# Half of w_out2 converted in the second phase, w_in over five batches, and the fifth transposition and first taps of the first batch ahead of val

## The chip, the cores and the metric

The kernel runs on one core of one Trainium2 chip. The metric is the device time of one execution in microseconds (us). The engines named are TensorE (PE), VectorE (DVE), ScalarE (ACT), GpSimd (POOL) and SyncE (SP), which issues all the DMAs.

## The reference

There are eight batches of 576 tokens by 512 features. Each batch goes through three layers:

```
kv   = k^T v per head;  o = q kv;  x = o / rms(o) * g_norm        # 8 heads of 64
gate = sigmoid(causal 5-tap convolution of x along the tokens)
y    = (gate * (x @ w_val)) @ w_out
h    = gelu(y @ w_in);  u, v = halves of h
v_s  = w_sg @ layernorm(v) + b_sg                                 # mixes the tokens of a batch
out  = y + (u * v_s) @ w_out2
```

The matrices w_val, w_out, w_in (512 x 1024) and w_out2 come in double precision.

## The kernel before, in words

**Products.** Each operand of a large product is split into a high and a low part, and a 128-row block of a result is twelve PE products (`gemm3`, L195 to L213: high by high, high by low, low by high, four slices of the contraction each). A weight is such a pair of tiles: WV for w_val, WO for w_out, wiv and wiu for the two halves of w_in, K and V for w_out2.

**Conversion of the weights.** Double precision arrives as pairs of 32-bit integers. `split` (L131) loads one piece (L148) and makes the parts with a chain over several engines: ACT L117 and DVE L127, then DVE L128 and L120, ACT L162 (the high part), DVE L129 and L124, POOL L167 (DVE for the first weights), DVE L169 (the low part). A piece of w_in or w_out2 is 128 x 256; w_in has 16 pieces, w_out2 has 8. Their raw integers lie in the two buffers of `raw`, their temporaries in the one buffer of `cv`. The phase-2 loads of tokens (L425) and of the gathered tokens (L541) take the same two buffers of `raw`.

**Phase 1**, per batch: kv (L252), o (L268) in five steps of 128 tokens (the fifth has 64), the root mean square (DVE L275 and L278, POOL L279 and L280), its scaling (DVE L283), the transposition on PE (L298), whose result ACT copies to the high part X0h or X1h (L302) and to X (L303) and DVE makes the low part of (L307); the convolution (`taps`: ACT L326; `conv`: DVE L332, sixteen instructions per batch), the sigmoid (ACT L335), `val` (PE L201, `val<-X0h,WV`), the gate (DVE L360, ACT L361, DVE or POOL L364), `out` (PE L201, `y<-Z,WO`), ACT L378 and the store to y_main (L380). The last 64 tokens of four batches are gathered and run as one more such block ("the rest", XR and GR).

**Phase 2**, per batch: the tokens of y are loaded back (L425), split by ACT L428 and DVE L429, multiplied with the v half of w_in (`hv`, PE L451), go through the gelu (ACT L436 and L440, DVE L437 and L441) and the normalisation (DVE L460 to L466, POOL L463, DVE L492); the u half is `hu`. `sg` (PE L560) mixes tokens, its eviction (DVE L561) scales and adds b_sg, which the tile bsg holds; `gated` (DVE L571, ACT L572, DVE L576) and `wout2` (PE L201, `out<-Z,K`) follow. X and `rem` belong to the remaining 64 tokens of each batch (ACT L519, DVE L520).

**What sets the order.** The opening, up to the second conversion of w_out, is written out by hand (L666 to L726). `busy(n)` there issues n idle products on PE (`warm`, two instructions each). After it the program is a list of closures: `later(slots, fn, rank)` puts one behind the next matrix products, `tick` runs those that are due, and `behind(marks, fn)` ties a conversion behind instructions that were issued three steps ago; a scheduler then orders each engine's queue. In batches 2 to 5 each odd step s converts one piece of w_in (L766). w_out2 takes the odd steps of batch 6 and steps 0 to 3 of batch 7 (L771 to L780). `background(pieces, every, first)` (L609) converts a list one by one, every so many ticks.

Of the kernel before, what the change touches and what calls it, by code (L numbers as in the profile page):

```python
# [10 lines left out]
F32R = mybir.dt.float32r  # L11
# [8 lines left out]
P = 128  # L20
B, S, D, DH = 8, 576, 512, 64
NK = D // P
# [38 lines left out]
def body(ctx, tc, qT, k, v, gcol, w_val, conv_w, w_out, w_in, g_ln, w_sgT, b_sg, w_out2, out, out_r):  # L61
# [8 lines left out]
    def sb(tag, shape, dtype=F32, bufs=1):  # L70
        count[0] += 1
        return pool.tile([P] + shape, dtype, tag=tag, name=f"{tag}_{count[0]}", bufs=bufs)
# [117 lines left out]
                for c in range(0, n, WC) for kt in range(NK)]  # L190

    wv = sb("WV", [2, NK, D], F32R)
    wo = sb("WO", [2, NK, D], F32R)

    def gemm3(ps, w, m, xh, xl):  # L195

        msl = slice(m * P, (m + 1) * P)
        i = 0
        for kt in range(NK):
            for a, x in ((w[0], xh), (w[1], xh), (w[0], xl)):  # L200
                nc.tensor.matmul(ps, lhsT=a[:, kt, msl], rhs=x[:, kt],  # L201
                                 start=(i == 0), stop=(i == 3 * NK - 1))
                i += 1
# [11 lines left out]
    def busy(n):  # L215
        for i in range(n):
            nc.tensor.matmul(warm[:, :P], lhsT=ident, rhs=ident, start=True, stop=True)
# [126 lines left out]
    class Moe:  # L344
# [26 lines left out]
        def out(self, m):  # L371
            if m == 0:
                self.y = sb("Y", [NK, self.n])
            ps = bank("y", self.n)
            gemm3(ps, (wo[:, 0], wo[:, 1]), m, self.z[:, 0], self.z[:, 1])

            def done():
                act(self.y[:, m], ps, AF.Copy)  # L378
                if m == NK - 1:
                    dma(self.dst, self.y)  # L380

            later(0, done, 1)
# [247 lines left out]
    spare = sb("Y", [2, 2 * D], I32)  # L630

    def first_weight(w, src, raws):
        return [split(src[:, m * P:(m + 1) * P], w[:, 0, :, m * P:(m + 1) * P], w[:, 1, :, m * P:(m + 1) * P],
                      raws[m], first[1][:, m % 2], NK, False)
                for m in range(NK)]

    wv_pieces = first_weight(wv, w_val, [first[0][:, i] for i in range(4)])
    wo_pieces = first_weight(wo, w_out, [spare[:, 0], spare[:, 1], first[0][:, 0], first[0][:, 1]])
    att = Attention(0)
    atts = [att, Attention(1)]  # L640
# [25 lines left out]
    with tc.manual_schedule():  # L666
        for m in range(NK):
            wv_pieces[m][0]()
        wo_pieces[0][0]()
        att.load_kv()  # L670
        dma(gcol_s, gcol)
        dma(gln_s, g_ln)
        cw_work = taps()
        att.load_q()
        atts[1].load_kv()
        wo_pieces[1][0]()
        atts[1].load_q()
        in_turn(wv_pieces[0], wv_pieces[1])
        in_turn(wv_pieces[2], wv_pieces[3])
        wo_pieces[2][0]()  # L680
        wo_pieces[3][0]()
        busy(27)
        att.kv(0)
        busy(5)
        att.kv(1)
        busy(4)
        in_turn(wo_pieces[0])
        slots.drain()
        cw_work()
        steps = [att.o(t, None) for t in range(5)]  # L690
        lows = []
        for t in range(5):
            steps[t][0](ts)
            if t >= 2:
                steps[t - 2][1]()
                busy(4)
                lows.append(steps[t - 2][2]())
            if t == 4:
                lows[0]()
        for t in (3, 4):  # L700
            steps[t][1]()
            if t == 3:
                busy(4)
                lows.append(steps[t][2]())
            lows[t - 2]()
        lows[3]()
        moe = Moe(att.xh, att.xl, gate, y_main[0])
        z = [moe.val(0, True)]
        steps[4][2]()
        for m in range(NK):  # L710
            att.taps(m)
        z.append(moe.val(1, True))
        atts[1].kv(0)
        atts[1].kv(1)
        slots.drain()
        z += [moe.val(m, True) for m in (2, 3)]
        for a in (0, 2):
            att.conv((a, a + 1))
            att.sigmoid(a)
            att.sigmoid(a + 1)  # L720
        for m in range(NK):
            z[m][0]()
        for m in range(NK):
            z[m][1](False)
        in_turn(wo_pieces[1])
    marks = [latest()]  # L726
    atts.append(Attention(2))
    atts[2].load_kv()

    for b in range(B):  # L730
        if b:
            moe = Moe(atts[b].xh, atts[b].xl, gate, y_main[b])
        nxt = atts[b + 1] if b + 1 < B else None
        nn = atts[b + 2] if b + 2 < B else None
        if b == 2:
            p2["wiv"], p2["wiu"] = (sb(n, [2, NK, D], F32R) for n in ("wiv", "wiu"))
            wi = split_weight(p2["wiv"], w_in, D, D) + split_weight(p2["wiu"], w_in, 0, D)
            wi[0][0]()
            wi[1][0]()
            wi_n = 0  # L740
        for s in range(8):
            if s < 4:
                if b:
                    moe.val(s)
            else:
                moe.out(s - 4)
            if b == 0 and s in (3, 4):
                later(0, lambda s=s: behind(marks[0], wo_pieces[s - 1][1]), 3)
            if b == 0 and s < 2:
                nxt.o(s)  # L750
            if nxt and s < 3:
                nxt.o(s + 2)
            if nn and s in (3, 4):
                nn.kv(s - 3)
            if nn and s == 3:
                nn.load_q()
            if b + 3 < B and s == 5:
                atts.append(Attention(b + 3))
                atts[-1].load_kv()
            if nn and s in (6, 7):  # L760
                nn.o(s - 6)
            if nxt and s in (5, 7):
                later(0, lambda a=nxt, m=s - 5: a.gates((m, m + 1)), 2)
            if s == 2:
                later(0, atts[b].rest_parts, 2)
            if b in (2, 3, 4, 5) and s % 2:  # L766
                later(0, lambda w=wi[wi_n][1], m=marks[-3]: behind(m, w), 3)
                if wi_n + 2 < len(wi):
                    later(0, wi[wi_n + 2][0], 4)
                wi_n += 1  # L770
            if b == B - 2 and s == 0:  # L771
                w2 = w2_pieces()
                w2[0][0]()
                w2[1][0]()
                w2_n = 0
            if (b == B - 2 and s % 2) or (b == B - 1 and s < 4):
                later(0, lambda w=w2[w2_n][1], m=marks[-3]: behind(m, w), 3)
                if w2_n + 2 < len(w2):
                    later(0, w2[w2_n + 2][0], 4)
                w2_n += 1  # L780
            if b == B - 1:
                if s == 0:
                    v_alloc()
                if s == 4:
                    stage = sb("X32", [NK, S])
                    dma(stage, w_sgT[:4 * P, :].rearrange("(t p) s -> p t s", p=P))
                    toks = Tokens(0)
                    toks.load(0)
                if s > 4:
                    toks.load(s - 4)  # L790
                    later(0, lambda t=s - 5: toks.split(t), 1)
            tick()
            marks.append(latest())
        if b % RG == RG - 1:
            moe = Moe(rest["x"][:, 0], rest["x"][:, 1], rest["g"], y_rest[b // RG])
            for s in range(8):
                if s < 4:
                    moe.val(s)
                else:
                    moe.out(s - 4)  # L800
                if b == B - 1:
                    if s == 0:
                        toks.split(3)
                    if s < 4:
                        toks.hv(s)
                    if s == 2:
                        rem = Rests(0)
                        later(1, rem.split, 1)
                    if s == 4:
                        sg_weight(stage)  # L810
                        rest_weight()
                        p2["r"] = sb("X32", [2, 2, D], F32R)
                        p2["bsg"] = sb("cv", [S])
                        dma(p2["bsg"], b_sg.to_broadcast([P, S]))
                    if s == 5:
                        y_r = Group.load(0)
                if b == B - 1 or s % 2:
                    tick()

    rem = rem.hv()  # L820
    grp = Group(0, y_r)
    tick()
    for b in range(B):
        more = b + 1 < B
        if b % RG == 0:
            if b:
                grp = Group(b // RG, Group.load(b // RG))
            ggr = sb("WO", [2, NK, RW], F32R)
            for m in range(NK):
                grp.hu(m)  # L830
                tick()
# [88 lines left out]
```

## Time and profile before

| | before |
|---|---|
| median of 3 runs | 770.35 us (769.9 to 770.45) |
| the profiled execution | 770.46 us |
| its span in the trace | 768.7 us |
| mean granted TensorE clock | 0.979 |
| busy: PE, DVE, ACT, POOL | 734.5, 589.6, 348.6, 152.7 us |

The busy times are sums over the span, which holds stages with different limits: the opening (to some 40 us), the first two batches (to some 100 us), the other batches of phase 1, the passage to phase 2 (at some 325 to 335 us) and phase 2. A row of the timeline has the start, the duration, the engine, the line, the operation and its tiles, and in brackets the time that the engine sat idle before and what ended it. The granted clock stands as a share of 2.4 GHz.

### The profile page before, as it was taken

How to read it: one execution, taken by the hardware profiler on the slowest of the kernel's cores; microseconds unless marked ns; L12 is line 12 of the kernel's file. 1: busy time of each engine (PE TensorE's matmuls, PEld its weight loads, DVE VectorE, ACT ScalarE, POOL GpSimd, SP SyncE). 2: the span in 40 equal slices, each digit the busy share in tenths (PEclk: the TensorE clock that was granted, in tenths of full speed). 3: DMA queues.
4: the chain of work that ended last, by engine and by line, in shares of the span. 5: the costliest groups of instructions: out<-in, count | busy, mean ns of one | idle time of the engine just before them, and what ended most of it. 6: DMA issues, size and time to landing. Idle time of an engine off the chain costs nothing.

```text
span 768.7 us, 11720 instructions
## 1 busy us (share of the span) xinstructions
PE 734.5 (96%) x4472; PEld 630.0 (82%) x4472; DVE 589.6 (77%) x1137; ACT 348.6 (45%) x662; POOL 152.7 (20%) x163
## 2 busy tenths in 40 slices
PE   6897999999899999859999999999999999999997
PEld 6785878778778787759988988889899888898896
DVE  7799959898779899759976687776875867867662
ACT  3567455655545765526543343433432423434320
POOL 0404425282344462311100000000000000100000
PEclk8998999999999999979999999999999999999999
DMA  9944153536134311342122022121321221121203
GB/s 298 319 136 174 55 181 109 185 123 206 59 129 163 104 69 69 127 144 92 60 61 104 28 70 83 55 79 38 118 91 47 70 96 43 67 70 42 96 1 110
DMA packets 56200, 80.15 MB, mean 104 GB/s; under 512 B 3664, under 2 KB 29264, under 8 KB 55120
## 3 DMA queue, kind: packets, MB, share of 16 engines
q1 hardware_dynamic: 56144, 79.40, 30.8%
q8 instruction: 35, 0.57, 0.3%
q14 instruction: 21, 0.17, 0.1%
HBM read 60.51 MB, written 18.87 MB: 103 GB/s over the span
## 4 chain that ended last, share of the span: by engine, by line
PE 83%; DVE 8%; DMA 4%; POOL 2%; issue 1%; ACT 1%; SPq 0%; DVEq 0%; POOLq 0%
PE sg L560 16%; PE hv L451 13%; PE out L201 12%; PE hu L201 11%; PE val L201 11%; PE y L201 10%; DVE G L332 4%; PE kv L252 3%; PE o L268 3%; PE xT L298 2%; PE hur L201 1%; DMA V<-in_v_dram 1%; DMA Q<-in_qT_dram 1%; POOL st L280 1%; DMA raw<-in_w_in_dram 1%
## 5 line engine op out<-in xcount | busy, mean ns | idle before, releaser
L201 PE MATMUL y<-Z,WO 128*128 128x512 f32 (+1 forms) x480 | 115.8, 389 | 3.0 <-DVE WO L169 2.8
L332 DVE SCALAR_TENSOR_TENSOR G<-X,cw,G 128x576 f32<-128x576 f32 x128 | 99.5, 821 | 9.2 <-ACT G L326 9.2
L201 PEld LDWEIGHTS y<-Z,WO 128*128 128x128 f32 x480 | 84.3, 194 | 20.1 <-DVE WO L169 3.2
L451 PE MATMUL hv<-wiv,X1h 128*128 128x512 f32 x256 | 84.0, 394 | 10.1 <-ACT X1h L428 10.1
L463 POOL TENSOR_TENSOR bmv<-bmv,mhalf 128x1 f32<-128x1 f32 x36 | 21.7, 603 | 348.2 <-DVE bmv L462 337.5
L201 PE MATMUL out<-Z,K 128*128 128x512 f32 x256 | 82.9, 389 | 0.0
L201 PE MATMUL hu<-X1h,wiu 128*128 128x512 f32 x256 | 79.5, 391 | 0.0
L280 POOL TENSOR_TENSOR st<-st,mhalf 128x8 f32<-128x8 f32 (+1 forms) x40 | 69.9, 1754 | 25.4 <-DVE st L279 23.0
L440 ACT ACTIVATE T<-T 128x512 f32<-128x512 f32 x68 | 42.9, 631 | 52.3 <-DVE T L437 52.2
L451 PEld LDWEIGHTS hv<-wiv,X1h 128*128 128x128 f32 x256 | 48.4, 190 | 20.1 <-ACT X1h L428 10.5
L201 PEld LDWEIGHTS out<-Z,K 128*128 128x128 f32 x256 | 48.1, 188 | 10.0
L201 PEld LDWEIGHTS hu<-X1h,wiu 128*128 128x128 f32 x256 | 46.6, 188 | 8.3
L561 DVE SCALAR_TENSOR_TENSOR T<-sg,gln,cv 128x288 f32<-128x288 f32 x64 | 32.8, 516 | 26.2 <-PE sg L560 25.8
L572 ACT ACTIVATE Z<-T 128x512 fp32r<-128x512 f32 x32 | 20.2, 632 | 67.3 <-DVE T L571 67.3
L451 PE MATMUL hv<-wiv,X1l 128*128 128x512 f32 x128 | 50.4, 394 | 0.0
L201 PE MATMUL hu<-X1l,wiu 128*128 128x512 f32 x128 | 50.1, 391 | 0.0
L201 PE MATMUL out<-Z,V 128*128 128x512 f32 x128 | 49.8, 389 | 0.0
L268 PEld LDWEIGHTS o<-kvbd,Q 128*128 128x128 f32 (+1 forms) x320 | 39.4, 180 | 5.8 <-issue 1.8
L201 PE MATMUL val<-X0h,WV 128*128 128x512 f32 x128 | 42.4, 412 | 0.8 <-ACT X0h L302 0.8
L268 PE MATMUL o<-kvbd,Q 128*128 128x128 f32 (+1 forms) x320 | 41.5, 275 | 0.9 <-DMA Q<-in_qT_dram 0.9
L201 PE MATMUL val<-X1h,WV 128*128 128x512 f32 x128 | 41.3, 403 | 0.0
L252 PEld LDWEIGHTS kv<-V,K 128*64 128x64 f32 (+1 forms) x640 | 26.3, 142 | 14.5 <-issue 11.4
(150 smaller groups left out, 1654.8 us busy)
## 6 DMA issues: line engine op xcount, KB each, us to landing
Q<-in_qT_dram SPq DMA_DIRECT2D x8, 1152.0 KB, 5.5
y_main<-Y SPq DMA_DIRECT2D x8, 1024.0 KB, 3.9
raw<-y_main SPq DMA_DIRECT2D x32, 256.0 KB, 3.1
Y<-y_main SPq DMA_DIRECT2D x32, 256.0 KB, 4.0
out_dram<-Y SPq DMA_DIRECT2D x32, 256.0 KB, 2.3
K<-in_k_dram SPq DMA_DIRECT2D x7, 1024.0 KB, 5.6
V<-in_v_dram SPq DMA_DIRECT2D x7, 1024.0 KB, 8.7
raw<-in_w_in_dram SPq DMA_DIRECT2D x16, 256.0 KB, 5.4
```

What stands on the lines that cost most here:

```text
L201: nc.tensor.matmul(ps, lhsT=a[:, kt, msl], rhs=x[:, kt], start=(i == 0), stop=(i == 3 * NK - 1))
L252: nc.tensor.matmul(self.pk[j][h, h], lhsT=self.k[:n, t, js][:, h], rhs=self.v[:n, t, js][:, h], start=(t == 0), stop=(t == 4))
L268: nc.tensor.matmul(po[:n, j * P:(j + 1) * P], lhsT=self.q[:, j, o:o + n], rhs=bd[:, j, :], start=True, stop=True)
L280: nc.gpsimd.tensor_tensor(st[:n, 2], st[:n, 1], mhalf[:n], op=ALU.pow)
L298: nc.tensor.transpose(pt[:, j * P:j * P + n], xo[:n, j * P:(j + 1) * P], ident[:n, :n])
L332: stt(gate[:, m], x32[:, m, j:j + S], cw3[:, m, j:j + 1], gate[:, m], op0=ALU.mult, op1=ALU.add)
L440: act(w, w, AF.Tanh, scale=CG * AG)
L451: nc.tensor.matmul(ps, lhsT=a[:, kt], rhs=p2["wiv"][:, w, kt], start=(i == 0), stop=(i == 3 * NK - 1))
L463: nc.gpsimd.tensor_tensor(mv[:, 3:4], mv[:, 2:3], mhalf[:, 0:1], op=ALU.pow)
L560: nc.tensor.matmul(ps, lhsT=a[:, msl], rhs=w, start=(n == 0), stop=(n == len(mm) - 1))
L561: later(0, lambda: stt(vs[:, sl], ps, gln_s[:, m:m + 1], p2["bsg"][:, sl], op0=ALU.mult, op1=ALU.add))
L572: act(g[:, 0], x, AF.Copy)
```

## The change

The tile WO becomes two tiles, WOh and WOl, so that in phase 2 the gated rest (ggr) takes only WOh, and bsg moves from `cv`, which stays free for conversions, to WOl. The idle products ahead of kv go from 27 to 40. In the opening the transposition of the fifth step and the taps stand ahead of val of the first batch. w_in is converted over batches 2 to 6, four pieces of w_out2 behind it in the steps left, and the other four in phase 2, from the end of the last rest block on.

```diff
-    wo = sb("WO", [2, NK, D], F32R)
+    wo = [sb(f"WO{i}", [NK, D], F32R) for i in "hl"]
...
-        busy(27)
+        busy(40)
         att.kv(0)
...
-        z = [moe.val(0, True)]
         steps[4][2]()
         for m in range(NK):
             att.taps(m)
-        z.append(moe.val(1, True))
+        z = [moe.val(m, True) for m in (0, 1)]
...
-            if b in (2, 3, 4, 5) and s % 2:
+            if (b, s) == (B - 3, 7):
+                w2 = w2_pieces()
+                wi += w2[:4]
+            if s in {2: (1, 4, 7), 3: odd, 4: odd, 5: odd, 6: odd, 7: (0,)}.get(b, ()):
                 later(0, lambda w=wi[wi_n][1], m=marks[-3]: behind(m, w), 3)
                 if wi_n + 2 < len(wi):
                     later(0, wi[wi_n + 2][0], 4)
                 wi_n += 1
-            if b == B - 2 and s == 0:
-                w2 = w2_pieces()
...
-            if (b == B - 2 and s % 2) or (b == B - 1 and s < 4):
-                later(0, lambda w=w2[w2_n][1], m=marks[-3]: behind(m, w), 3)
...
-                        p2["bsg"] = sb("cv", [S])
-                        dma(p2["bsg"], b_sg.to_broadcast([P, S]))
                     if s == 5:
                         y_r = Group.load(0)
+                    if s == 6:
+                        background(w2[4:], 2, 2)
...
     grp = Group(0, y_r)
+    p2["bsg"] = sb("WOl", [S])
+    dma(p2["bsg"], b_sg.to_broadcast([P, S]))
...
-            ggr = sb("WO", [2, NK, RW], F32R)
+            ggr = sb("WOh", [2, NK, RW], F32R)
```

On PE, at the end of the opening, the order before is this (T_297 is the fourth step's block of 128 tokens, T_305 the fifth's of 64; val_376 and val_400 are the first two blocks of val):

```order
L298 MATMUL xT_364<-ident_65,T_297 128x128 x4
L201 MATMUL val_376<-X0h_90,WV_79 128x512 x2
L201 MATMUL val_376<-X0l_91,WV_79 128x512
...
L201 MATMUL val_376<-X0l_91,WV_79 128x512
L298 MATMUL xT_390<-ident_65,T_305 128x64 x4
L201 MATMUL val_400<-X0h_90,WV_79 128x512 x2
```

And now, with T_311 the fourth and T_319 the fifth step's block:

```order
L298 MATMUL xT_378<-ident_65,T_311 128x128 x4
L298 MATMUL xT_389<-ident_65,T_319 128x64 x4
L201 MATMUL val_400<-X0h_91,WV_79 128x512 x2
L201 MATMUL val_400<-X0l_92,WV_79 128x512
...
L201 MATMUL val_400<-X0l_92,WV_79 128x512
L201 MATMUL val_414<-X0h_91,WV_79 128x512 x2
```

The last transposition has moved from behind twelve products to ahead of them.

On SP, at the passage to phase 2, the order before is this (raw<-in_w_out are pieces of w_out2, raw<-y_main the first tokens of phase 2):

```order
L786 DMA X_412_3070<-in_w_sgT_dram 128x4x576
L148 DMA raw_2814<-in_w_out_dram 128x512
L148 DMA raw_2880<-in_w_out_dram 128x512
L148 DMA raw_2933<-in_w_out_dram 128x512
L148 DMA raw_2968<-in_w_out_dram 128x512
L380 DMA y_main<-Y_3056 128x2048
L148 DMA raw_2997<-in_w_out_dram 128x512
L425 DMA raw_3074<-y_main 128x4x128
L425 DMA raw_3090<-y_main 128x4x128
```

And now:

```order
L779 DMA X_405_3036<-in_w_sgT_dram 128x4x576
L148 DMA raw_2816<-in_w_out_dram 128x512
L148 DMA raw_2882<-in_w_out_dram 128x512
L425 DMA raw_3040<-y_main 128x4x128
L425 DMA raw_3056<-y_main 128x4x128
L425 DMA raw_3074<-y_main 128x4x128
L380 DMA y_main<-Y_3022 128x2048
```

Three loads of pieces have left the queue ahead of the first tokens, and the store of the last batch of phase 1 stands behind three of them.

On DVE, in the first batch of phase 2, the order now has these rows ahead of the first eviction of sg (X_448 belongs to the remaining tokens, cv_3450 is the second and cv_3496 the third of the late pieces); before, L520 and L561 stood there with no conversion between them:

```order
L124 SCALAR_TENSOR_TENSOR cv_3450<-raw_3392,cv_3450 128x256
L520 TENSOR_TENSOR X_448_3302<-T_3377,X_448_3302 64x512
L169 TENSOR_TENSOR V_2630<-cv_3450 128x256
L520 TENSOR_TENSOR X_448_3302<-T_3377,X_448_3302 64x512
L127 TENSOR_SCALAR cv_3496<-raw_3448 128x256
L128 TENSOR_SCALAR cv_3496<-cv_3496 128x256
L120 SCALAR_TENSOR_TENSOR cv_3496<-cv_3496 128x256
L129 TENSOR_SCALAR cv_3496<-cv_3496 128x256
L124 SCALAR_TENSOR_TENSOR cv_3496<-raw_3448,cv_3496 128x256
L169 TENSOR_TENSOR V_2630<-cv_3496 128x256
L561 SCALAR_TENSOR_TENSOR T_3525<-sg_3526,gln_77,WOl_3386 128x288
```

One whole piece has come between the subtraction for the remaining tokens and the first eviction; of the piece before it the last two instructions lie around that subtraction.

## Rows read from the trace of the kernel before

**Rows 1.** Page, part 1: busy us, share of the span, instructions.

```profile
PE 734.5 (96%) x4472; PEld 630.0 (82%) x4472; DVE 589.6 (77%) x1137; ACT 348.6 (45%) x662; POOL 152.7 (20%) x163
```

**Rows 2.** Page, part 4: the chain of waits, shares by engine.

```profile
PE 83%; DVE 8%; DMA 4%; POOL 2%; issue 1%; ACT 1%; SPq 0%; DVEq 0%; POOLq 0%
```

**Rows 3.** Timeline of PE: three of the places where it waited.

```profile
22.42 4.83 PE L268 MATMUL o<-kvbd,Q 128*128 128x128 f32 x40 [0.86 <-DMA Q<-in_qT_dram]
...
76.49 1.97 PE L201 MATMUL y<-Z,WO 128*128 128x512 f32 x5 [2.78 <-DVE WO L169]
...
334.75 0.79 PE L451 MATMUL hv<-wiv,X1h 128*128 128x512 f32 x1 [10.07 <-ACT X1h L428]
```

**Rows 4.** Windows: length; busy PE, PEld, DVE, ACT, POOL; clock; DMA share; GB/s.

```profile
39.83:101.70 61.87, 56.38 (x440) 46.02 (x438) 58.44 (x94) 34.77 (x64) 25.52 (x22) 0.92 0.38 132
101.70:193.00 91.30, 90.72 (x633) 73.14 (x632) 74.61 (x131) 52.90 (x100) 38.16 (x35) 1.00 0.46 156
193.00:199.00 6.00, 2.41 (x19) 2.03 (x19) 6.00 (x13) 3.48 (x8) 3.12 (x4) 1.00 0.00 0
324.70:334.75 10.05, 0.00 (x0) 0.00 (x0) 6.36 (x18) 3.60 (x9) 2.46 (x4) 0.75 0.52 183
334.75:340.00 5.25, 5.25 (x18) 4.71 (x19) 2.67 (x4) 0.89 (x2) 0.88 (x1) 0.50 0.50 149
340.00:400.00 60.00, 60.00 (x369) 54.40 (x368) 49.61 (x103) 31.86 (x65) 5.65 (x6) 1.00 0.25 77
400.00:757.00 357.00, 357.00 (x1939) 314.51 (x1938) 254.49 (x512) 131.27 (x242) 16.76 (x31) 1.00 0.20 66
```

**Rows 5.** Timeline of PE: the idle products at the start and the first kv.

```profile
2.27 7.81 PE L217 MATMUL warm<-ident 128*128 128x128 f32 x54 [2.27 <-POOL X L207]
14.04 1.97 PE L252 MATMUL kv<-V,K 128*64 128x64 f32 x32 [3.96 <-DMA V<-in_v_dram]
```

**Rows 6.** Timeline: from the fifth step's scaling to the first convolution.

```profile
33.38 0.68 DVE L283 TENSOR_TENSOR T<-o,st 64x512 f32<-64x512 f32 x1 [0.24 <-POOL st L280]
...
35.43 0.51 PE L201 MATMUL val<-X0l,WV 128*128 128x512 f32 x1 [0.68 <-DVE X0l L307]
...
37.97 0.46 PE L298 MATMUL xT<-ident,T 64*128 64x64 f32 x4
...
39.83 1.55 DVE L332 SCALAR_TENSOR_TENSOR G<-X,cw,G 128x576 f32<-128x576 f32 x2 [4.45 <-ACT G L326]
```

**Rows 7.** Timeline of DVE: its longest waits between 39.83 and 101.70 us.

```profile
63.08 0.69 DVE L283 TENSOR_TENSOR T<-o,st 128x512 f32<-128x512 f32 x1 [0.93 <-POOL st L280]
...
65.63 0.69 DVE L283 TENSOR_TENSOR T<-o,st 128x512 f32<-128x512 f32 x1 [0.87 <-POOL st L280]
...
95.20 0.69 DVE L360 TENSOR_TENSOR T<-val,G 128x512 f32<-128x512 f32 x1 [0.92 <-PE val L201]
```

**Rows 8.** Timeline: starts of two conversions, and loads that freed buffers released.

```profile
320.57 4.06 SPq L148 DMA_DIRECT2D raw<-in_w_out_dram  x2
321.60 0.29 DVE L127 TENSOR_SCALAR cv<-raw 128x256 int32<-128x256 int32 x1
...
325.35 0.29 DVE L127 TENSOR_SCALAR cv<-raw 128x256 int32<-128x256 int32 x1
...
330.97 5.03 SPq L425 DMA_DIRECT2D raw<-y_main  x2
```

**Rows 9.** Timeline: phase 2, the remaining tokens, sg that reads them, batch 1's first hv.

```profile
374.13 1.41 DVE L520 TENSOR_TENSOR X<-T,X 64x512 fp32r<-64x512 f32 x2 [0.17 <-ACT X L519]
...
376.10 0.68 PE L560 MATMUL sg<-WV,X 128*128 128x288 f32 x4
...
392.48 0.62 PE L451 MATMUL hv<-wiv,X1h 128*128 128x512 f32 x2
```

**Rows 10.** Timeline of POOL: two powers of one kind.

```profile
350.38 0.55 POOL L463 TENSOR_TENSOR bmv<-bmv,mhalf 128x1 f32<-128x1 f32 x1
353.98 2.34 POOL L463 TENSOR_TENSOR bmv<-bmv,mhalf 128x1 f32<-128x1 f32 x1 [3.06 <-DVE bmv L462]
```

More of the change, by code (lines that the diff above doesn't have):

```diff
@@ L374, in out @@
             ps = bank("y", self.n)
-            gemm3(ps, (wo[:, 0], wo[:, 1]), m, self.z[:, 0], self.z[:, 1])
+            gemm3(ps, wo, m, self.z[:, 0], self.z[:, 1])
             def done():
@@ L632, in first_weight @@
     def first_weight(w, src, raws):
-        return [split(src[:, m * P:(m + 1) * P], w[:, 0, :, m * P:(m + 1) * P], w[:, 1, :, m * P:(m + 1) * P],
+        return [split(src[:, m * P:(m + 1) * P], w[0][:, :, m * P:(m + 1) * P], w[1][:, :, m * P:(m + 1) * P],
                       raws[m], first[1][:, m % 2], NK, False)
                 for m in range(NK)]
-    wv_pieces = first_weight(wv, w_val, [first[0][:, i] for i in range(4)])
+    wv_pieces = first_weight((wv[:, 0], wv[:, 1]), w_val, [first[0][:, i] for i in range(4)])
     wo_pieces = first_weight(wo, w_out, [spare[:, 0], spare[:, 1], first[0][:, 0], first[0][:, 1]])
@@ L728, in body @@
     atts[2].load_kv()
+    odd = (1, 3, 5, 7)
     for b in range(B):
@@ L770, in body @@
                 wi_n += 1
-            if b == B - 2 and s == 0:
-                w2 = w2_pieces()
-                w2[0][0]()
-                w2[1][0]()
-                w2_n = 0
-            if (b == B - 2 and s % 2) or (b == B - 1 and s < 4):
-                later(0, lambda w=w2[w2_n][1], m=marks[-3]: behind(m, w), 3)
-                if w2_n + 2 < len(w2):
-                    later(0, w2[w2_n + 2][0], 4)
-                w2_n += 1
             if b == B - 1:
```

## The prediction

> **What bounds the kernel now.** I read the page's busy times first, then the shares of the chain of waits, then the timeline of PE for every place where it sat idle, then windows around these places. PE is busy 734.5 of 768.7 us [rows 1] and holds 83% of the chain, DVE 8%, DMA 4%, POOL 2% [rows 2]: whatever this change gives must come out of the few places where PE waits, or where its clock is low after a wait. The reader is to see these places in the timeline [rows 3]: 0.86 us ahead of the first o (a load of Q), 2.78 in the out of batch 0 (DVE), and 10.07 ahead of the first hv. Windows say what the neighbours do there [rows 4]. From 39.83 to 101.70 DVE is busy 58.44 of 61.87 us, and PE only 56.38, at a mean granted clock of 0.92: DVE bounds this stretch. From 101.70 to 193 PE is busy 90.72 of 91.30 and DVE 74.61: PE bounds it. From 193 to 199 PE is busy 2.41 of 6.00 and DVE 6.00 of 6.00. In the passage, 324.70 to 334.75, PE does nothing, and right behind it, 334.75 to 340.00, it runs at the granted clock of 0.50, its lower level of 1.2 GHz. From 340 to 400 and from 400 to 757 it is busy without a gap at the full clock of 2.4 GHz, with DVE at 49.61 of 60 and 254.49 of 357.
>
> **The change part by part.** The sum is made against the profiled execution's 770.46 us (span 768.7 and 1.76 around it); the median of the runs is 770.35, 0.1 lower, so the two can be taken as one.
>
> *Idle products.* 27 of them take 7.81 us and end at 10.08; kv starts at 14.04, when V lands [rows 5]. One takes 7.81 / 27 = 0.289 us; 13 more take 3.76 and end at 13.84, still 0.2 ahead of V, so they cost nothing. If they ran at half the clock throughout (0.58 us each) they would end 13 x 0.58 = 7.5 us later, at 17.6, and kv would be 3.6 late; the first 27 show no such price, so I take 0. I count no gain either: a quicker kv is followed by o, which waited for Q's load until 22.42 [rows 3], and that load does not move.
>
> *The fifth transposition.* Before, the fifth block is scaled by 33.38 + 0.68 = 34.06, but its transposition stands behind twelve products of val and starts at 37.97; the first convolution follows at 39.83, 1.86 later [rows 6]. Val itself had to wait for X0l until 35.43 with its second kind of product [rows 6], so PE has room ahead of it. Now the transposition can start about 34.2, the convolution about 34.2 + 1.86 = 36.06, 3.8 us earlier. The val products behind it are late by the 0.46 us of the transposition; nobody waits for them before the convolution is through, twelve instructions of which follow. The wait that this removes is DVE's, 4.45 us [rows 6].
>
> *What 3.8 us on DVE become.* DVE bounds the stretch to the end of batch 1's first out, so it carries the 3.8 on. Besides, the new order puts DVE's reductions for the second batch ahead of all scalings, with pieces of w_out between: the two waits for POOL's powers, 0.93 and 0.87, can close, and so can 0.92 for a val that PE brought late because it had itself stood at WO [rows 3, 7]. That makes 3.8 + 0.93 + 0.87 + 0.92 = 6.5. The ends: 3.8, if these waits stay, and 3.8 + (61.87 - 58.44) = 7.2, if DVE loses all its idle time of the window. PE can follow, since it has 61.87 - 56.38 = 5.5 us of idle and 8% of low clock in the window. I take 6.5, nearest to the rows of the single waits. Behind 101.70 PE is the bound and passes it on whole; the wait at 193 to 199 stays, since batch 3 has its four pieces as before and DVE stood in no queue from before (74.61 of 91.30) [rows 4].
>
> *The passage.* Before, six pieces of w_out2 stand on DVE behind the last convolution, now three. One takes 3.1 to 3.75 us from start to start (321.60 to 325.35) [rows 8]. More weighty than DVE is the raw buffer: the first tokens' load stood behind the last pieces and was issued at 330.97, when the fifth piece of the six let its buffer go; hv started 3.78 us later. Now it takes the buffer that the second of them frees, the one that at 320.57 released two loads of pieces [rows 8]. So it comes at 320.57 + 3.78 = 324.35 where PE is free at 324.70: the wait of 10.07 goes [rows 3]. The low clock behind it goes as well: 5.25 us of work at half the clock are 2.6 at the full one [rows 4]. What is late next is the second block of tokens, behind the third piece in the other buffer; the rest's products fill most of that, and I give 0.5 back. Sum: -10.07 - 2.6 + 0.5 = -12.2. If the tokens came as late as one piece (3.75) and the clock stayed low for it, -10.07 + 3.75 = -6.3; if nothing came late at all, -12.7.
>
> *Four pieces in the first batch of phase 2.* The passage's DVE time, 6.36 us for 18 instructions, is three pieces less a fraction [rows 4]; one piece is 6 instructions, 2.1 us of DVE, four are 8.5. From 340 to 400 DVE had 60 - 49.61 = 10.4 us to spare [rows 4], so they fit as a mean, with PE as cover. But two places are tight: the subtraction for the remaining tokens ends at 374.13 + 1.41 = 375.54, and sg reads it at 376.10 [rows 9], a slack of 0.6; and a whole piece, some 3 us with its waits for ACT and POOL, now stands ahead of the first eviction of sg. PE can go on into further banks meanwhile. From below: 0, all hidden. From above: four pieces in the open at 3.6 each, 14.4. I take 2, near to hidden, since PE's order has other products beside sg there.
>
> *Order of the rest.* bsg in WOl and ggr in WOh add no instructions; w_in's last pieces in batches 6 and 7 lie under PE, which is busy there as in 101.70 to 193 [rows 4]. 0.
>
> Sum: 770.46 - 6.5 - 12.2 + 2 = 753.8 us.
>
> **The rivals.**
> 1. *The opening gives little.* The 3.8 us end at a product that waits for a converted piece of w_out: PE stood 2.78 at WO [rows 3], and its conversion moves with DVE's queue only if the scheduler leaves it in place. For it: two waits stand in that stretch, both on DVE; against: the pieces are on the same DVE, which starts earlier. If nothing is left of the 6.5, 760.3 us.
> 2. *The late pieces lie in the open.* All four delay sg or what feeds it: 753.8 + 14.4 - 2 = 766.2. For it: the slack of 0.6 [rows 9]; against: 10.4 spare us of DVE [rows 4].
> 3. *POOL is slowed beside the conversions.* One power of a column took 0.55 us and another 2.34 [rows 10]. Five such powers of the first batch at the slow price cost 5 x (2.34 - 0.55) = 9, where the normalised tokens are waited for: 763. For it: the conversion's two-operand instructions now run beside these powers; against: the slow one is a single row of the first batch of phase 2, and POOL was busy 5.65 of 60 us [rows 4]. The Trainium skill ("GPSIMD Engine Reference", section 8, Key points) says that GpSimd shares its SBUF interfaces with VectorE, with contention against VectorE instructions that have two SBUF inputs; by that rule a power beside L124, L120 or L169 would be slowed. The two powers of this trace agree in that such a spread exists, but do not show what ran beside them as its cause.
> 4. *Slower: the tokens of batch 1 queue behind the late pieces.* The raw buffers are two, and SP issues in order: the loads of the third and fourth piece stand ahead of the tokens of batch 1. The third piece's chain stands behind the subtraction that ends at 375.54 and takes some 3.1 us, so its buffer comes free at 378.6 in the times of the trace before; batch 1's hv is at 392.48 [rows 9], and less the 3.78 us from issue to use its load has to leave at 388.7. If DVE is late by more than these 10 us in that batch, each of four blocks of tokens waits up to 3.78 us, 15.1, and the clock falls as behind the wait at 334.75, 2.6: 753.8 + 15.1 + 2.6 = 771.5. DVE has 10.4 to spare and 8.5 to take in [rows 4], so it would need rival 3 as well.
>
> **How the numbers follow.** The forecast has 0.62; rival 1 0.15, rival 2 0.10, rival 3 0.08, rival 4 0.05. The forecast's own spread is -7.2 to -3.8 and -12.7 to -6.3 in the two gains, and 0 to 5 in the late pieces, not all at once: 748 to 760. The range of 746 to 765 takes in rivals 1 and 3 and leaves out rivals 2 and 4: both gains at their best are 770.46 - 7.2 - 12.7 = 750.6, and 746 would have most of the wait at 193 to 199 gone too. A measurement of this kernel can tell about 0.2%, 1.5 us, from no change. Faster by more: the forecast, rivals 1 to 3 but for a tail of two of them together, 0.93. Within: 0.03, where rivals 1 and 2 meet (770.46 - 12.2 + 14.4 = 772.7 at their worst, and 769 with three of the four pieces in the open). Slower: rival 4 and such sums, 0.04.
>
> **What would show it.** Idle products end below 14.04 and kv still starts at V's landing. The first convolution starts about 36. DVE's waits at L283 for the powers shrink, PE's wait at WO goes, and batch 1's first out comes 6 to 7 us earlier. hv of phase 2 starts with under 1 us of idle, and no window at clock 0.50 follows. In the first batch of phase 2, waits of PE at sg add up to 2 us or less, and the powers at L463 keep near 0.55. It is wrong if the convolution starts early but out does not, if hv still waits for X1h, if PE has waits of over 4 us at sg, or if hv of batch 1 waits for tokens.

## The result and the profile after

| | before | changed |
|---|---|---|
| median | 770.4 us (769.9 to 771.04, 4 runs) | 751.29 us (750.8 to 752.53, 4 runs) |
| ratio | | 0.9755, 95% interval 0.974 to 0.9769 |
| the profiled execution, its span | 770.46 us, 768.7 us | 752.53 us, 750.8 us |
| mean granted clock | 0.979 | 0.991 |
| sum of PE's idle time (span less busy) | 34.2 us | 20.2 us |

The forecast was 753.8 us, the range 746 to 765. The changed kernel's profiled execution is the slowest of its four; the three others have clocks of 0.995 to 0.997. The page's busy times and chain after:

```profile
PE 730.6 (97%) x4498; PEld 628.4 (84%) x4498; DVE 589.0 (78%) x1137; ACT 348.5 (46%) x662; POOL 152.1 (20%) x163
```

```profile
PE 82%; DVE 9%; DMA 3%; POOL 2%; issue 1%; ACT 1%; SPq 1%; DVEq 0%; POOLq 0%
```

The shares hardly differ from [rows 1, 2], though 19 us are gone: shares of a whole span don't show such a change. The view of PE's waits does (what waited, for what; us in total, times, longest):

```profile
PE xT L298 <- DVE T L283: 7.1, 8, 2.0
PE warm L217 <- POOL X L207: 2.3, 1, 2.3
PE kv L252 <- DMA V<-in_v_dram: 2.3, 3, 1.3
PE o L268 <- DMA Q<-in_qT_dram: 1.6, 1, 1.6
```

The two waits of [rows 3] that the change was to meet, 2.78 at y and 10.07 at hv, are not in the list. At the passage the timeline after reads so (SP's issue, ACT's copy, the first hv):

```profile
314.72 5.56 SPq L425 DMA_DIRECT2D raw<-y_main  x3
...
317.68 0.63 ACT L428 ACTIVATE X1h<-raw 128x512 fp32r<-128x512 f32 x1 [0.39 <-DMA raw<-y_main]
...
318.66 0.40 PE L451 MATMUL hv<-wiv,X1h 128*128 128x512 f32 x1
```

The load leaves when a piece frees a buffer (its L124 ends at 314.65), and hv starts 3.94 us later with no idle time in front of it; before it was 330.97 and 334.75 [rows 3, 8]. Windows after, columns as in [rows 4]:

```profile
36.00:101.00 65.00, 61.45 (x509) 49.72 (x510) 61.37 (x98) 39.36 (x72) 26.21 (x22) 1.00 0.41 139
101.00:185.00 84.00, 83.81 (x565) 67.75 (x564) 72.67 (x127) 50.00 (x94) 34.96 (x33) 1.00 0.51 169
185.00:195.00 10.00, 6.47 (x52) 6.09 (x51) 9.97 (x20) 5.91 (x13) 4.97 (x6) 0.96 0.01 2
340.00:382.00 42.00, 42.00 (x257) 38.23 (x256) 39.80 (x96) 22.70 (x50) 5.09 (x7) 1.00 0.29 93
382.00:740.00 358.00, 358.00 (x1949) 315.51 (x1948) 255.31 (x515) 131.28 (x243) 16.80 (x31) 1.00 0.21 67
```

The first batches run at the full clock, 1.00 where it was 0.92. The first batch of phase 2 takes the four late pieces: DVE is busy 39.80 of 42 us, and PE all 42 at the full clock. The waits at the end of batch 3 are nearly as they were, 1.57 and 1.96 us where 1.66 and 1.93 stood before, on the rows that answer to PE's waits in the 193 to 199 window of [rows 4]:

```profile
189.16 0.63 PE L298 MATMUL xT<-ident,T 128*128 128x128 f32 x4 [1.57 <-DVE T L283]
192.93 0.66 PE L298 MATMUL xT<-ident,T 128*128 128x128 f32 x4 [1.96 <-DVE T L283]
```

### The profile page after: what moved, and what is told of

The parts are those of the page before. It is cut to its first block, busy times and chain, and to the rows that moved or that the text cites. A ratio compares the mean times of both kernels' runs of the same rounds, so it can differ in the third digit from the quotient of the medians.

```text
span 750.8 us, 11758 instructions
## 1 busy us (share of the span) xinstructions
PE 730.6 (97%) x4498; PEld 628.4 (84%) x4498; DVE 589.0 (78%) x1137; ACT 348.5 (46%) x662; POOL 152.1 (20%) x163
## 4 chain that ended last, share of the span: by engine, by line
PE 82%; DVE 9%; DMA 3%; POOL 2%; issue 1%; ACT 1%; SPq 1%; DVEq 0%; POOLq 0%
PE sg L560 16%; PE hv L451 13%; PE out L201 12%; PE hu L201 12%; PE val L201 10%; PE y L201 9%; DVE G L332 5%; PE kv L252 3%; PE o L268 3%; PE xT L298 2%; POOL st L280 2%; PE hur L201 2%; DMA Q<-in_qT_dram 1%; DMA V<-in_v_dram 1%; DVE st L278 1%
## 5 line engine op out<-in xcount | busy, mean ns | idle before, releaser
L201 PE MATMUL y<-Z,WOh 128*128 128x512 f32 (+1 forms) x320 | 100.5, 384 | 0.0
L463 POOL TENSOR_TENSOR bmv<-bmv,mhalf 128x1 f32<-128x1 f32 x36 | 21.5, 597 | 345.1 <-DVE bmv L462 345.1
L280 POOL TENSOR_TENSOR st<-st,mhalf 128x8 f32<-128x8 f32 (+1 forms) x40 | 74.2, 1862 | 27.4 <-DVE st L279 24.9
L201 PEld LDWEIGHTS y<-Z,WOh 128*128 128x128 f32 x320 | 58.2, 189 | 11.3
L201 PE MATMUL y<-Z,WOl 128*128 128x512 f32 (+1 forms) x160 | 59.4, 373 | 0.0
L561 DVE SCALAR_TENSOR_TENSOR T<-sg,gln,WOl 128x288 f32<-128x288 f32 x64 | 32.7, 516 | 26.5 <-PE sg L560 26.2
L268 PEld LDWEIGHTS o<-kvbd,Q 128*128 128x128 f32 (+1 forms) x320 | 41.0, 188 | 6.5 <-ACT kvbd L261 1.8
L268 PE MATMUL o<-kvbd,Q 128*128 128x128 f32 (+1 forms) x320 | 43.1, 283 | 1.6 <-DMA Q<-in_qT_dram 1.6
```

What stands on the lines that cost most here:

```text
L201: nc.tensor.matmul(ps, lhsT=a[:, kt, msl], rhs=x[:, kt], start=(i == 0), stop=(i == 3 * NK - 1))
L268: nc.tensor.matmul(po[:n, j * P:(j + 1) * P], lhsT=self.q[:, j, o:o + n], rhs=bd[:, j, :], start=True, stop=True)
L280: nc.gpsimd.tensor_tensor(st[:n, 2], st[:n, 1], mhalf[:n], op=ALU.pow)
L463: nc.gpsimd.tensor_tensor(mv[:, 3:4], mv[:, 2:3], mhalf[:, 0:1], op=ALU.pow)
L561: later(0, lambda: stt(vs[:, sl], ps, gln_s[:, m:m + 1], p2["bsg"][:, sl], op0=ALU.mult, op1=ALU.add))
```

## Experiments

Each was timed in five rounds against the kernel before, in three groups: e1 to e4 (before: 769.9 us), e5 to e8 (770.62) and e9 to e12 (770.43).

| kernel | median us | ratio, 95% interval |
|---|---|---|
| e1, changed, 27 idle products | 752.66 | 0.9786 (0.977 to 0.9802) |
| e2, changed, old opening | 756.61 | 0.9839 (0.982 to 0.9858) |
| e3, before, new opening | 765.73 | 0.9951 (0.9937 to 0.9965) |
| e4, pieces (and tiles) alone | 758.36 | 0.985 (0.9836 to 0.9863) |
| e5, before, tokens in a tile of their own | 771.09 | 1.0009 (0.9999 to 1.0019) |
| e6, all eight pieces in phase 1 | 766.47 | 0.9947 (0.9932 to 0.9961) |
| e7, all eight pieces in phase 2 | 764.77 | 0.9926 (0.9914 to 0.9939) |
| e8, fewer pieces in batch 3 | 751.3 | 0.9756 (0.9741 to 0.9771) |
| e9, the changed kernel again | 750.02 | 0.974 (0.9719 to 0.976) |
| e10, more idle products ahead of o | 750.6 | 0.9742 (0.9722 to 0.9763) |
| e11, before, new opening, two tiles | 765.58 | 0.9932 (0.9914 to 0.9951) |
| e12, e8 and e10 together | 750.35 | 0.9736 (0.9715 to 0.9758) |

**e3 and e11: the opening alone.** e3's edit on the kernel before is the one of the change (transposition and taps ahead of the first val); e11 adds the tiles WOh and WOl.

> The kernel before with the new opening order alone: one tile WO, 27 idle products, all conversions as before. Theory: 770.4 - 6 = 764.4 us, PE's wait of 10 us at hv stays. Rival (the split of WO did it): 770.4 - 0 to 2 = 768.4 to 770.4.

> The kernel before with the new opening order and WO as two tiles, 27 idle products, conversions as before. The opening alone gave 4.2 us, less than the 6.5 forecast. Theory 1 (the two tiles let w_out's conversions run earlier and give the missing 1.5): 764.2. Theory 2 (the missing part comes with the fewer pieces of batch 2): 765.7, as the opening alone.

e3 gave 4.2 us, e11 4.9: the two tiles are worth nothing that can be told. In e3 the first convolution starts at 36.34, and hv still waits 10.0 us. DVE's waits behind it (its longest up to 100 us):

```profile
36.34 3.01 DVE L332 SCALAR_TENSOR_TENSOR G<-X,cw,G 128x576 f32<-128x576 f32 x4 [0.67 <-ACT G L326]
...
52.07 0.69 DVE L360 TENSOR_TENSOR T<-val,G 128x512 f32<-128x512 f32 x1 [1.85 <-PE val L201]
...
86.42 0.69 DVE L283 TENSOR_TENSOR T<-o,st 128x512 f32<-128x512 f32 x1 [1.53 <-POOL st L280]
```

The waits of [rows 7] are gone, but a val (1.85) and another power (1.53) have opened in their place: 3.49 us came at the first convolution, and in this trace nothing was added behind it.

**e2 and e4: the pieces alone.**

```diff
-        steps[4][2]()
-        for m in range(NK):
-            att.taps(m)
-        z = [moe.val(m, True) for m in (0, 1)]
+        z = [moe.val(0, True)]
+        steps[4][2]()
+        for m in range(NK):
+            att.taps(m)
+        z.append(moe.val(1, True))
```

e4 has this and `busy(27)`, e2 has it alone.

> The changed kernel with the old opening and 27 idle products: the conversions moved, WO as two tiles, nothing else. Theory (the passage gives 12.5 us, and the late pieces cost nothing): 770.4 - 12.5 = 758 us, no wait at hv. Rival (the gains are not separate, the opening's is passed on only because the conversions of batches 2 to 5 are fewer): 754 or less, so that this and the opening alone don't add up to 19.

> The changed kernel with the opening's order of before: fifth transposition and taps behind the first val. Theory (the opening's order gives some 6 us, 3.8 at the first convolution and the rest at waits of DVE and PE behind it): 757 to 758 us, the convolution later by about 3.8 and PE's wait at the converted w_out back. Rival (the two tiles WOh and WOl let y start earlier, and that is what the opening gained): within 1.5 us of the changed kernel, 751 to 753.

e4 gave 11.5 us; its wait at hv is 0.2 us in all. From e4 to e1 the opening is worth 758.36 - 752.66 = 5.7, from e2 to the changed kernel 5.3, or 6.6 against its second measurement (e9). So the opening is worth a little more where the pieces have moved (5.3 to 6.6) than alone (4.2 to 4.9).

**e1 and e9: the idle products.** e1 is the changed kernel with `busy(27)`, e9 the changed kernel itself.

> The changed kernel with 27 idle products ahead of kv instead of 40. Theory (idle products cost and give nothing, since kv waits for V's load and o for Q's): no change against the changed kernel's 751.3 us, within 1 us. Rival (the 13 products keep the granted clock up over the first kv and o): slower by 1 to 3 us, with more of the stretch from 14 to 28 us at a low clock.

> The changed kernel itself, beside the others of this group. If the 40 idle products are worth something, it is below the 752.7 us that the same kernel had with 27; theory (they are worth nothing): the two agree within 0.5 us. Expected by the first result: 751.3.

The 13 products are worth something: 752.66 (751.94 to 754.51) with 27, against 751.29 and 750.02 with 40. It is little: the intervals of the ratios, 0.977 to 0.9802 against 0.974 to 0.9769 and 0.9719 to 0.976, only just miss each other. It is not the start that pays. The first o and the first convolution of e1:

```profile
22.82 4.83 PE L268 MATMUL o<-kvbd,Q 128*128 128x128 f32 x40 [1.12 <-DMA Q<-in_qT_dram]
...
36.45 3.01 DVE L332 SCALAR_TENSOR_TENSOR G<-X,cw,G 128x576 f32<-128x576 f32 x4 [0.67 <-ACT G L326]
...
72.16 0.50 PE L201 MATMUL y<-Z,WOl 128*128 128x512 f32 x1 [2.14 <-DVE WOl L169]
```

And of the changed kernel, where the third row's wait is gone (the last two rows are the first products of that out on either side of the gap):

```profile
23.45 6.55 PE L268 MATMUL o<-kvbd,Q 128*128 128x128 f32 x40 [1.57 <-DMA Q<-in_qT_dram]
...
38.07 3.00 DVE L332 SCALAR_TENSOR_TENSOR G<-X,cw,G 128x576 f32<-128x576 f32 x4 [0.47 <-ACT G L326]
...
71.10 0.50 PE L201 MATMUL y<-Z,WOh 128*128 128x512 f32 x1
...
76.92 0.39 PE L201 MATMUL y<-Z,WOl 128*128 128x512 f32 x1
```

With 40 the convolution even starts later here, since o ran at a low clock (0.68 from 22 to 30 us), but y's wait of 2.14 for the converted w_out is gone. The order on PE tells why: behind the opening the scheduler now puts three blocks of o and products of val between the first product of an out (71.10) and the one that needs the new WOl (76.92). With 27 the latter comes straight after one block of o. That the scheduler does so because it counts the idle products as time of PE is an inference. So 13 idle products reordered batch 0: the three traces with the new opening and 27 of them (e1, e3, e11) wait 2.1 to 2.2 us there, and none with the new opening and 40 does. That this reordering is the whole of the 1.4 to 2.6 us is not shown: e2 and e4 differ by the idle products too, 1.75 us, and both wait at WOl in their traces (2.68 and 2.19).

**e5: the tokens' buffer.**

```diff
+                    tokq = sb("Q", [4, NK, P])
                     v_alloc()
...
-                    toks.load(0)
+                    toks.load(0, tokq[:, 0])
...
-                    toks.load(s - 4)
+                    toks.load(s - 4, tokq[:, s - 4])
```

`load` then hands this tile to `load_piece` in place of a buffer of raw.

> The kernel before, with one thing changed: the first batch's four blocks of tokens are loaded into the tile Q, idle by then, and not into the two buffers of raw. The same eight pieces of w_out2 are made, and they are issued at the same steps. Theory (the wait of 10 us at hv is the tokens' load queued for a raw buffer, not the work of the pieces on DVE): hv waits under 1 us, 770 - 12 = 758 us, with the pieces drifting in behind hv at no cost. Rival (DVE's work on the pieces sets hv): hv still waits 7 us or more, 766 to 770 us.

No gain, but the wait has moved. In e5 hv starts at 318.68 without a wait, 16 us earlier than before. The next users of raw are the gathered tokens of the rest, and these now wait for the pieces:

```profile
340.87 0.41 DVE L124 SCALAR_TENSOR_TENSOR cv<-raw,cv 128x256 f32<-128x256 uint32 x1
341.34 0.56 SPq L425 DMA_DIRECT2D raw<-y_rest  x1
...
349.43 4.30 PE L451 MATMUL hv<-wiv,kvbd 128*128 128x512 f32 x11 [3.73 <-DVE kvbd L429]
...
359.43 0.80 PE L201 MATMUL hur<-XR,wiu 128*128 128x256 f32 x2 [5.70 <-ACT XR L534]
```

3.73 + 5.70 = 9.4 us, near to the 10.07 before, and the granted clock is low behind both (0.72 from 349 to 355 and again from 359 to 366 us). The piece's last reading instruction (L124) at 340.87 frees the buffer, the load leaves at 341.34. So the queue for the two buffers is the cause of the first hv's wait, which is shown; but to lift it for four loads gives nothing while the pieces still stand ahead of the next ones. The forecast of 758 fell with that.

**e6 and e7: all pieces on one side.** e6 converts all eight in phase 1, with five in batch 7; e7 all eight in phase 2, one at each tick, behind the same last rest block. The two edits are put together here.

```diff
-                wi += w2[:4]
+                wi += w2                                # e6; e7 leaves it out
-            if s in {2: (1, 4, 7), 3: odd, 4: odd, 5: odd, 6: odd, 7: (0,)}.get(b, ()):
+            if s in {2: (1, 4, 7), 3: odd, 4: odd, 5: odd, 6: odd, 7: (0, 1, 2, 3, 4)}.get(b, ()):   # e6
+            if s in {2: (1, 4, 7), 3: odd, 4: odd, 5: odd, 6: (1,)}.get(b, ()):                      # e7
-                        background(w2[4:], 2, 2)        # e6: none
+                        background(w2, 1, 1)            # e7
```

> The changed kernel with all eight pieces of w_out2 made in phase 1 (five of them in batch 7) and none in phase 2; opening, idle products and tiles as changed. Theory: four more pieces stand ahead of the tokens' load, 4 x 3.3 = 13 us later where 0.4 were to spare, and the low clock behind the wait costs 2.6 again: 764 to 767 us. Rival (the late pieces cost as much in phase 2 as they save at the passage): 751 to 755.

> The changed kernel with all eight pieces of w_out2 made in phase 2, one at each tick, none in phase 1. Theory (the late pieces cost nothing as long as DVE's time beside PE covers them): eight need 17 us of DVE where the changed kernel's trace has 39.8 busy of 42 with four, so some 6 to 8 us come into the open at sg, out or the tokens of batch 1: 756 to 760 us. Rival (later always hides): 751.

e6 came out as forecast, 15 us slower than the changed kernel, with the tokens' load at 326.66 and a longer wait than before:

```profile
326.66 5.78 SPq L425 DMA_DIRECT2D raw<-y_main  x3
...
330.35 0.80 PE L451 MATMUL hv<-wiv,X1h 128*128 128x512 f32 x1 [13.06 <-ACT X1h L428]
```

e7 is 13.5 us slower, more than the 5 to 9 expected, and by another way than a shortage of DVE's time alone: the loads of five pieces stand in SP's queue from 353.17 on, each until a buffer is free, and the tokens of batch 1 behind them.

```profile
353.17 23.62 SPq L148 DMA_DIRECT2D raw<-in_w_out_dram  x5
379.56 10.61 SPq L425 DMA_DIRECT2D raw<-y_main  x4
```

```profile
383.41 0.79 PE L451 MATMUL hv<-wiv,X1h 128*128 128x512 f32 x1 [11.35 <-ACT X1h L428]
```

DVE is busy 39.13 of the 43 us from 340 to 383, so the pieces themselves come late and their loads with them. The tokens' load leaves at 379.56, when the last piece but one frees its buffer, and hv starts 3.85 later: the wait of the passage once more, one batch on. The clock falls as well, to 0.50 from 383 to 389 us.

**e8, e10 and e12: further versions.** e8 converts w_in at steps `{2: odd, 3: (1, 3, 5), ...}`, e10 puts `busy(9)` for `busy(4)` behind the second kv, e12 does both.

> The changed kernel with the pieces of w_in in batch 2 at steps 1, 3, 5, 7 and in batch 3 at 1, 3, 5: none at batch 3's last step. Theory (the waits of 1.57 and 1.96 us of PE at the end of batch 3 stand behind a DVE that is busy without a gap, a piece among its work): one piece less there frees 2.1 us of DVE, the waits shrink by 2 to 3.5 us and the low clock behind them by up to 1.7: 747 to 749 us. Rival (the powers on POOL and the convolution set these waits): 751, the waits as they are.

> The changed kernel with 9 idle products instead of 4 between the second kv and o, which fill the 1.6 us in which PE waited for Q. Theory (in the changed kernel's profiled execution o fell to the low clock, 6.55 us in place of 4.83, after such a wait, and the first convolution came 1.6 us late by it): o at the full clock, 749.5 to 750.5 us. Rival (where the low clock falls at the start differs from execution to execution and idle products do not decide it): 751.3.

> The changed kernel with both: 9 idle products ahead of o, and the pieces of batches 2 and 3 at steps 1, 3, 5, 7 and 1, 3, 5. The second alone left the median at 751.3. Theory: 749.5 to 750.5 us, by the idle products alone; rival: 751.3, neither does anything.

None of them can be told from the changed kernel. In e8 the waits at the end of batch 3 stand as before:

```profile
187.83 0.63 PE L298 MATMUL xT<-ident,T 128*128 128x128 f32 x4 [1.58 <-ACT G L335]
...
191.59 0.66 PE L298 MATMUL xT<-ident,T 128*128 128x128 f32 x4 [1.96 <-DVE T L283]
```

Its trace still has the steps of a piece on DVE in this stretch (L120 at 183.22, L129 at 188.35, L124 at 192.52), so whether a piece among DVE's work causes these waits was not tested by it and stays open. In e10 o ran 4.75 us without a wait, as meant, and the convolution came at 37.06; the profiled execution was still 753.02 us, the slowest of its five. In e9 o took 7.02 us, the convolution came at 36.87, and it was 749.75. So o's duration does not decide the time of these two executions: in e9 o could start at 21.77, in e10 at 23.50.

**The stages of six profiled executions.** The starts of four events cut each trace into stages: the first convolution, the second wait of PE at the end of batch 3, the first hv of phase 2, and the end of the span.

| us | before | e3 | e4 | e1 | changed | e9 |
|---|---|---|---|---|---|---|
| start to first convolution | 39.83 | 36.34 | 40.44 | 36.45 | 38.07 | 36.87 |
| to the wait at the end of batch 3 | 158.92 | 159.26 | 156.95 | 156.16 | 154.86 | 154.86 |
| to the first hv | 136.00 | 135.98 | 125.74 | 125.75 | 125.73 | 124.19 |
| to the end | 434.0 | 433.8 | 432.2 | 432.5 | 432.1 | 432.0 |

The rows at the end of batch 3, in the order before, e3, e4, e1, e9 (that of the changed kernel, 192.93, is shown above), and the first hv of e4 and e9:

```profile
198.75 0.66 PE L298 MATMUL xT<-ident,T 128*128 128x128 f32 x4 [1.93 <-DVE T L283]
...
195.60 0.66 PE L298 MATMUL xT<-ident,T 128*128 128x128 f32 x4 [1.98 <-DVE T L283]
...
197.39 0.66 PE L298 MATMUL xT<-ident,T 128*128 128x128 f32 x4 [1.98 <-DVE T L283]
...
192.61 0.66 PE L298 MATMUL xT<-ident,T 128*128 128x128 f32 x4 [1.93 <-DVE T L283]
...
191.73 0.66 PE L298 MATMUL xT<-ident,T 128*128 128x128 f32 x4 [1.93 <-DVE T L283]
```

```profile
323.13 0.40 PE L451 MATMUL hv<-wiv,X1h 128*128 128x512 f32 x1
...
315.92 0.39 PE L451 MATMUL hv<-wiv,X1h 128*128 128x512 f32 x1
```

The second stage is 1.30 us shorter with 40 idle products than with 27 (e1), by the same amount in both traces of the changed kernel. One trace of e1 stands against two here, and a low clock can hide as much: e10 has 40 of these products too, and its second stage took 156.3 at a clock of 0.97 from 36 to 101 us. These two traces of one kernel differ by 1.20 us at the start and by 1.54 behind the wait of batch 3, where the granted clock is 0.72 in the first (192.9 to 199 us) and 1.00 in the second (191.7 to 198). The opening alone (e3) does not shorten the second stage; the pieces with the two tiles (e4) shorten it by 2.0.

## Why the prediction was right

**The passage, -12.2: right in mechanism and size.** Alone (e4) it gave 11.5 us, with the late pieces in it. In e4's trace the stage ahead of hv is 10.3 us shorter than before and the one behind it 1.8. One row was misread: of the two loads in the row of 320.57 [rows 8] only the first left then, the second at 324.31; the sum does not change by it. The price per piece held: back with four pieces ahead of the tokens (e6), 15 us came back, 13.06 of them at hv.

**The late pieces, +2: they cost 0.** PE was busy 42.00 of 42 us in that stretch. The slack of 0.6 at the remaining tokens did not bind, as PE had other products. The forecast left no more than 2 us there, so this term was 2 us too dear.

**The opening, -6.5: too large.** The 3.8 at the first convolution came: DVE's wait there fell from 4.45 to 0.67 in e3, and the convolution started 3.5 earlier (39.83 to 36.34), the fifth block being scaled 0.3 later in that execution. But the step that added 0.93 + 0.87 + 0.92 for three waits that close failed: they closed, and others of the same kind opened (1.85 and 1.53 in e3; 0.51, 1.53 and 1.07 in the changed kernel). A stretch that DVE bounds at 58.44 of 61.87 has its last 3 us in waits that belong to the chain through POOL and PE, and these move with the work. Batch 1's first out came 3.6 us earlier (101.67 to 98.04; in e9 4.8), not the 6 to 7 that were given as a sign. What came on top of 3.5, 0.7 to 2.2 us according to the kernel it is put in (3.1 against e9), I can only place near the clock: over 36 to 101 us it was 0.92 before and in e2, 0.95 in e3 and e4, 0.97 in e11, 1.00 in e1 and in the changed kernel. That is not shown as the cause.

**The idle products, 0: wrong by 1.4 to 2.6 us.** They were costed as instructions that hide behind V's load, which is true of them; what they do to the scheduler's order behind the opening was not looked at. The 1.30 us of the second stage are what the traces show of it.

**Order of the rest, 0: too small.** In e4, without the new opening, the stage from the first convolution to the end of batch 3 is 2.0 us shorter than before. Whether the fewer pieces in batch 2, the two tiles or the clock (0.95 against 0.92) did it was not separated.

**The sum.** -4.2 (e3), -11.5 (e4) and -1.4 to -2.6 make 752.1 to 753.3 from 770.4; measured were 751.29 and 750.02. The errors of the steps, +2.3 (opening), +0.7 (passage), -2 (pieces) and -1.4 to -2.6 (idle products), cancel in part: that the forecast of 753.8 is nearer than its terms is luck in part. The spread of 748 to 760 did not follow from its own bounds either: both gains at their best and free pieces make 750.6.

**The rivals.** The opening that gives little was out (e3's interval excludes no gain). The late pieces in the open were out with four pieces. The powers on POOL kept their median: after, the line of L463 has (duration ns, least, median, most)

```profile
L463 POOL TENSOR_TENSOR bmv<-bmv,mhalf x36: 538/543/2204, 329.5 to 702.7; 128x1 f32<-128x1 f32 x36
```

The median was 542 ns before. But a median hides the few slow ones, of which one took 2.34 us before [rows 10] and one 2.20 after, from 336.39 on. What VectorE did beside them, before (first row) and after:

```profile
353.82 2.08 DVE L406 TENSOR_TENSOR G<-X,WV 128x576 fp32r<-128x576 f32 x3
...
336.23 0.74 DVE L406 TENSOR_TENSOR G<-X,WV 128x576 fp32r<-128x576 f32 x1
336.90 1.28 DVE L535 TENSOR_TENSOR XR<-raw,XR 128x512 fp32r<-128x512 f32 x2
```

Each of these instructions has two inputs from SBUF, and each slow power ends 0.4 us behind the last of them. The next slowest power, 0.85 us in both traces, lies beside one such L492 of 0.68. The Trainium skill ("GPSIMD Engine Reference", section 8, Key points) has GpSimd contend with VectorE instructions of two SBUF inputs, and these rows agree with it. No conversion was the partner: the one power with a two-input row of a conversion beside it (L169 at 351.34, 0.42 us long) took 0.54, and PE had no wait in that stretch. So what this rival names is seen in both kernels, and its price did not come.

The slower rival, the tokens of batch 1 queued behind the late pieces, did not come with four pieces but is real: with eight (e7) it cost 11.35 us at one place plus the low clock, where 15.1 had been put for four blocks in turn.

## What to carry to other kernels

Where a load waits, look for who holds its buffer and what stands ahead of it in the issuing queue: the work itself (here 2.1 us of DVE per piece) may be free, while the place in the ring of two buffers costs some 3.3 us of waiting per piece (13.06 us for four, in e6). Moving a user off the ring moves the wait to the next user; moving the work to a stretch with PE as bound and DVE time to spare makes it free, until that stretch is full. A wait that is removed in a chain over three engines often opens the next one at once: count the first step of such a chain as gain, and the rest only if the new order shows that nothing else comes last there.

## What was not expected of the hardware and the order

Idle products ahead of a load changed the time by their effect on a scheduler's order many instructions later: 1.30 us in the second stage, and 1.4 to 2.6 in the medians, for 13 products that no engine waits for. And executions of one kernel differ in where the low clock falls: the same o took 6.55 and 7.02 us in two profiled executions of the changed kernel, 4.83 in e1, with total times of 752.53, 749.75 and 752.66 that don't follow it. Of the 2.9 us between the spans of the first two, 1.54 lie behind the wait of batch 3, where one ran at 0.72 and the other at full clock. A power of one column on GpSimd took 2.20 to 2.34 us in place of 0.54 while VectorE ran instructions with two SBUF inputs back to back beside it.
